# A retention and mixture-of-experts kernel on one core: a weight piece, a chunk's scaling and the last eviction are moved

## The chip, the cores and the metric

The kernel runs on one core of one Trainium2 chip. The metric is the device time of one execution in microseconds (us); the median of three timed executions before the change is 379.56 us (379.56 to 379.77).

## The reference

A retention layer (4 batches, 8 heads, 768 positions, head size 64) feeds a mixture of 8 experts. Every token goes to the one expert with the largest gate logit.

```python
for t in range(S):
    state = gamma[None, :, None, None] * state + np.einsum('bhd,bhe->bhde', k[:, :, t], v[:, :, t])
    y[:, :, t] = scale * np.einsum('bhd,bhde->bhe', q[:, :, t], state)
...
logits = x @ w_gate
expert_idx = np.argmax(logits, axis=1)
...
    h = np.maximum(xe @ w1[e], 0.0)
    ye = h @ w2[e]
    out[mask] = gate_w[mask, None] * ye
```

x is y with its heads side by side: 3072 tokens of 512 numbers. w1 is 512x1024 and w2 1024x512 for each expert.

## The kernel before

The work is written out by hand in one order; each engine executes its own instructions in the order in which the code issues them, and waits where data or a buffer is missing.

**Attention.** The 3072 tokens are 24 chunks of 128, taken two at a time in 12 periods (n = 0 to 11; period n has the chunks a = 2n and b = 2n+1). In a period TensorE adds the carried state to Y (`carry`), forms the gate logits of the period before (`logits`, `finish_logits`), turns that period's rows (`rows`), updates the state U (`update`), adds the chunk's own part to Y (`output`), and computes the next period's scores. VectorE evicts Y times a decay into xT (`evict`) and the masked scores into Sb. GpSimd scales v into vs (`scale`; chunk g's vs is read by `update(g)` and `output(g)`). Y has one buffer, so the carry of the next period waits until both evictions are done.

**Sending.** Once a chunk's slots are known, GpSimd sends its 128 rows to the expert regions of x_sorted in HBM by an indirect DMA (`send_apart`, one DMA for each chunk, with `between()` after each but the last; by default `between` is `pause`, a small multiplication whose result nobody reads). `soon` is period 9: there chunks 16 and 17 are sent, and SyncE then reads the first 240 rows of the first expert back (`fetch_early` into xg0), which can only start when every row sent so far has landed. In period 11 VectorE turns xg0 into xt (`turn_early`, L868), ScalarE casts it into xh (`cut_high`, L875), and TensorE starts the first expert's hidden layer with it (`fill`, L908).

**Weights.** Raw float32 weights are split into a high part (ScalarE, `whi`) and a rest (`wlo`) in pieces; SPLITS[7] are the three pieces of period 7, whose rests VectorE computes.

**Experts.** From about 98 us on TensorE runs the experts; the eighth one's last block of 120 tokens is computed in two halves of 256 columns (`last_rows`). Each half is evicted from its own bank of PSUM with the gate weight as a factor and sent to the output by GpSimd. The execution ends when the second of these DMAs has landed.

## Time and profile before

| | |
|---|---|
| timed executions | median 379.56 us, 379.56 to 379.77 |
| profiled execution | 379.4 us, span 377.6 us |
| TensorE (PE) busy | 371.0 us, 98% of the span |
| VectorE (DVE) busy | 251.7 us, 67% |
| GpSimd (POOL) busy | 260.3 us, 69% |
| ScalarE (ACT) busy | 140.5 us, 37% |
| granted TensorE clock | 0.997 of full speed |

The span runs from the first to the last instruction of the program; 1.8 us of the profiled execution lie around it. TensorE's ends are modelled, so that a short wait between two matmuls can be hidden in its busy time; the starts are recorded.

### The profile page before, as it was taken

Reading aid. Unit: us, or ns where it says so; the run is one execution under the profiler, and the core shown is the slowest. Engines: PE = TensorE matmul, PEld = TensorE weight load, DVE = VectorE, ACT = ScalarE, POOL = GpSimd, SP = SyncE. Lnnn points to the kernel's source line nnn. Section 1 sums busy time; section 2 is a strip of 40 time slices with the busy share of each in tenths; the row PEclk is TensorE's granted clock in tenths of the full one; section 3 lists DMA queues with packets and bytes.
Section 4 is the critical chain, followed back from the end, with each engine's and each line's share of the span. In section 5 each row is a group of like instructions: output and inputs, shape, how many; then the busy total and the mean of one; then the engine's idle time right before and its main releaser. Section 6 shows DMA issues by size and latency. Waiting matters only on the chain. (4 is left out here: it accounts for less than half of the span.)

```text
span 377.6 us, 8710 instructions
## 1 busy us (share of the span) xinstructions
PE 371.0 (98%) x3279; PEld 349.3 (93%) x3279; DVE 251.7 (67%) x496; ACT 140.5 (37%) x252; POOL 260.3 (69%) x278
## 2 busy tenths in 40 slices
PE   8999999999999999999999999999999999999994
PEld 5888888788899899999999999999999999999984
DVE  3467858877778866768784777576676668667211
ACT  2222344244541645534630543154235316424200
POOL 3751669988760299008996999499569929987873
PEclk9999999999999999999999999999999999999998
DMA  7999999986249597869646754846457557520102
GB/s 305 417 414 420 416 402 423 417 353 172 92 159 201 197 240 252 262 217 277 223 145 115 231 162 141 194 166 210 133 149 224 176 91 251 184 101 24 38 20 80
DMA packets 42031, 82.06 MB, mean 217 GB/s; under 512 B 4268, under 2 KB 17584, under 8 KB 39537
## 3 DMA queue, kind: packets, MB, share of 16 engines
q1 hardware_dynamic: 36656, 67.67, 54.4%
q0 software_dynamic: 5312, 13.49, 10.0%
q8 instruction: 47, 0.77, 0.9%
q14 instruction: 16, 0.12, 0.1%
HBM read 65.80 MB, written 15.85 MB: 216 GB/s over the span
## 5 line engine op out<-in xcount | busy, mean ns | idle before, releaser
L853 POOL DMA_INDIRECT out<-Z,sidx x88 | 100.9, 1147 | 63.9 <-DVE Z L1061 49.2
L148 DVE TENSOR_TENSOR wlo<-raw,whi 128x1024 fp32r<-128x1024 f32 (+1 forms) x63 | 74.0, 1178 | 16.5 <-ACT whi L147 16.2
L203 POOL TENSOR_TENSOR idle<-cs 1x256 bf16<-1x256 f32 x102 | 79.6, 780 | 2.8
L147 ACT CAST whi<-raw 128x1024 fp32r<-128x1024 f32 (+1 forms) x72 | 67.7, 951 | 5.8 <-DMA raw<-w 5.8
L1218 PE MATMUL py<-hh,whi 128*128 128x392 f32 (+4 forms) x192 | 65.7, 342 | 0.0
L1218 PE MATMUL py<-hl,whi 128*128 128x392 f32 (+4 forms) x192 | 65.7, 342 | 0.0
L1218 PE MATMUL py<-hh,wlo 128*128 128x392 f32 (+4 forms) x192 | 65.7, 342 | 0.0
L1193 ACT ACTIVATE hh<-ph 128x452 fp32r<-128x452 f32 (+6 forms) x56 | 28.4, 507 | 77.6 <-PE ph L1186 77.1
L1186 PE MATMUL ph<-xh,wlo 128*128 128x392 f32 (+5 forms) x224 | 49.0, 340 | 0.0
L1186 PE MATMUL ph<-xl,whi 128*128 128x392 f32 (+5 forms) x224 | 48.9, 340 | 0.0
L1186 PE MATMUL ph<-xh,whi 128*128 128x392 f32 (+5 forms) x224 | 48.9, 340 | 0.0
L1194 DVE SCALAR_TENSOR_TENSOR hl<-ph,hh 128x452 fp32r<-128x452 f32 (+6 forms) x56 | 32.1, 574 | 20.3 <-ACT hh L1193 19.5
L1186 PEld LDWEIGHTS ph<-xh,whi 128*128 128x128 f32 x224 | 40.2, 188 | 0.4
L1186 PEld LDWEIGHTS ph<-xl,whi 128*128 128x128 f32 x224 | 40.3, 188 | 0.2
L1186 PEld LDWEIGHTS ph<-xh,wlo 128*128 128x128 f32 x224 | 40.2, 188 | 0.1
L1218 PEld LDWEIGHTS py<-hl,whi 128*128 128x128 f32 x192 | 36.1, 188 | 0.2
L1218 PEld LDWEIGHTS py<-hh,wlo 128*128 128x128 f32 x192 | 36.1, 188 | 0.2
L1218 PEld LDWEIGHTS py<-hh,whi 128*128 128x128 f32 x192 | 36.0, 188 | 0.2
L287 DVE TENSOR_TENSOR Sb<-sp,cs 128x512 f32<-128x512 f32 x48 | 29.9, 681 | 5.9 <-PE sp L284 5.9
L875 ACT CAST xh<-buf 128x512 fp32r<-128x512 f32 (+6 forms) x24 | 13.3, 558 | 51.5 <-DVE buf L868 51.5
L853 POOL DMA_INDIRECT x_sorted<-xrow,KEY x24 | 24.9, 1037 | 6.9 <-issue 4.1
L1056 DVE STREAM_TRANSPOSE Z<-py 128x416 f32<-128x416 f32 (+3 forms) x24 | 15.0, 625 | 18.9 <-PE py L1218 18.5
(200 smaller groups left out, 555.6 us busy)
## 6 DMA issues: line engine op xcount, KB each, us to landing
raw<-w SPq DMA_DIRECT2D x32, 1024.0 KB, 6.1
qkv_w<-qkv SPq DMA_DIRECT2D x12, 1024.0 KB, 17.7
qkv_t<-qkv SPq DMA_DIRECT2D x7, 1024.0 KB, 15.1
qkv_t<-front SPq DMA_DIRECT2D x7, 512.0 KB, 7.5
buf<-x_sorted SPq DMA_DIRECT2D x12, 211.2 KB, 5.2
x_sorted<-cs SPq DMA_DIRECT2D x7, 260.0 KB, 5.5
buf<-x_sorted SPq DMA_DIRECT2D x8, 195.0 KB, 3.9
out<-Z,sidx POOLq DMA_INDIRECT x88, 3.6
```

What stands on the lines that cost most here:

```text
L147: nc.scalar.copy(out=hi[:, h], in_=raw[:, h])
L148: engine.tensor_tensor(out=lo[:, h], in0=raw[:, h], in1=hi[:, h].bitcast(F32), op=ALU.subtract)
L203: nc.gpsimd.tensor_tensor(out=idle[0:1], in0=cs[0:1, 0:PAUSE], in1=cs[0:1, 0:PAUSE], op=ALU.mult)
L287: nc.vector.tensor_tensor(out=Sb[:, r], in0=sps[r], in1=causal.unsqueeze(1).broadcast_to([P, NP, C]), op=ALU.mult)
L853: sc = tc.nc.gpsimd.indirect_dma_start(out=dst, out_offset=bass.IndirectOffsetOnAxis(ap=index, axis=0), in_=rows, in_offset=None, bounds_c ...
L875: nc.scalar.copy(out=xh[:, :, c0:c0 + w], in_=xt[:, :, t0:t0 + w])
L1056: nc.vector.transpose(out=Zs[e][:, 0:nb, k, :], in_=py[:, 0:32 * nb].rearrange("p (j c) -> p j c", c=32))
L1186: nc.tensor.matmul(out=ph[:, :w], lhsT=wparts[e, f // 4][a][:, kd, fo:fo + P], rhs=x[:, kd, :w], start=(n == 0), stop=(n == 3 * KD - 1))
L1193: nc.scalar.activation(out=hh[:, :cap], in_=ph[:, :cap], func=AF.Relu)
L1194: nc.vector.scalar_tensor_tensor(out=hl[:, :cap], in0=ph[:, :cap], scalar=0.0, in1=hh[:, :cap].bitcast(F32), op0=ALU.max, op1=ALU.subtract)
L1218: nc.tensor.matmul(out=py[:, :c], lhsT=a[:, f % 4, k * P:(k + 1) * P], rhs=x[:, :c], **se)
```

## The change

Three edits. In period 7 the third weight piece is split after the two evictions, where it was split before them. In period 9 the scaling of chunk 21 stands between the sends of chunks 16 and 17, where a pause stood; it stood behind the second send. And each half of the last eviction is shared: VectorE takes 128 of its 256 columns and ScalarE the other 128.

```diff
-            for i in SPLITS[n][1:] if n == 7 else ():
+            for i in SPLITS[n][1:2] if n == 7 else ():
                 split(0, *i, nc.vector, 1)
...
-                send_apart(range(FULL - 2, FULL))
+                send_apart(range(FULL - 2, FULL), lambda: scale(b + 2))
                 fill_late()
                 fetch_early()
...
             for g in (a, b):
                 evict(g)
+            for i in SPLITS[n][2:] if n == 7 else ():
+                split(0, *i, nc.vector, 1)
...
-                if n not in BEHIND:
+                if n not in BEHIND and n != soon:
                     scale(b + 2)
...
-            nc.vector.tensor_scalar(out=half.rearrange("p (o k r) -> p k o r", o=2, k=KD),
-                                    in0=py[:w, 0:DM // 2].rearrange("p (k o r) -> p k o r", o=2, k=KD),
-                                    scalar1=meta[:w, j, 1:2], scalar2=None, op0=ALU.mult)
+            src = py[:w, 0:DM // 2].rearrange("p (k o r) -> p k o r", o=2, k=KD)
+            dst = half.rearrange("p (o k r) -> p k o r", o=2, k=KD)
+            by = meta[:w, j, 1:2]
+            nc.vector.tensor_scalar(out=dst[:, :, 0], in0=src[:, :, 0], scalar1=by, scalar2=None, op0=ALU.mult)
+            nc.scalar.activation(out=dst[:, :, 1], in_=src[:, :, 1], func=AF.Copy, scale=by)
             scatter_rows(tc, out_halves, pair[:w, q:q + 1], half, "rows")
```

On VectorE, in period 7 (wlo is a weight piece's rest, xT an eviction of Y, Sb the masked scores):

```order
 L287 TENSOR_TENSOR Sb<-sp,cs 128x512 x4
 L408 TENSOR_REDUCE lg_1120<-lp 128x16
-L148 TENSOR_TENSOR wlo<-raw,whi 128x512 x3
-L345 TENSOR_TENSOR xT<-Y,buf 128x4x128 x2
+L148 TENSOR_TENSOR wlo<-raw,whi 128x512 x2
+L345 TENSOR_TENSOR xT<-Y,buf 128x4x128 x2
+L148 TENSOR_TENSOR wlo<-raw,whi 128x512
 L287 TENSOR_TENSOR Sb<-sp,cs 128x512 x4
 L408 TENSOR_REDUCE lg_1120<-lp 128x16
```

Both evictions stand one piece earlier; the scores' evictions still stand behind three pieces and two evictions.

On GpSimd, at the sends of chunks 15, 16 and 17, before (idle is the pause, vs a chunk's scaling):

```order
L853 DMA x_sorted<-xrow,KEY 25600x520
L203 TENSOR_TENSOR idle<-cs 1x256
L853 DMA x_sorted<-xrow,KEY 25600x520 x2
L203 TENSOR_TENSOR idle<-cs 1x256
L853 DMA x_sorted<-xrow,KEY 25600x520
L261 TENSOR_TENSOR vs<-qkv_t,cs 128x512 x2
L148 TENSOR_TENSOR wlo<-raw,whi 128x512 x2
```

and of the change:

```order
L203 TENSOR_TENSOR idle<-cs 1x256
L855 DMA x_sorted<-xrow,KEY 25600x520 x2
L261 TENSOR_TENSOR vs<-qkv_t,cs 128x512
L855 DMA x_sorted<-xrow,KEY 25600x520
L261 TENSOR_TENSOR vs<-qkv_t,cs 128x512
L148 TENSOR_TENSOR wlo<-raw,whi 128x512 x2
```

The pause in front of the last of these sends (chunk 17) is gone, and the first of the two scalings (chunk 21) stands in its place.

On ScalarE, at the program's end, of the change, each row with the engines whose semaphores it waits for (hh is the hidden layer, yo the output rows, py the bank of PSUM):

```order
L1197 ACTIVATE hh<-ph_2196 128x376 [waits DVE_49,PE_49]
L1046 ACTIVATE yo<-py_2192,meta_97 120x128 [waits DMASW4_49,DVE_49]
L1046 ACTIVATE yo<-py_2193,meta_97 120x128 [waits DVE_49]
L841 TENSOR_LOAD top [waits DVE_49]
L842 COMPARE_AND_BRANCH
```

and on GpSimd, there, of the change:

```order
L855 DMA out<-yo,sidx_101 3072x512 [waits DMASW4_49,DVE_49]
L203 TENSOR_TENSOR idle<-cs 1x256 [waits Pool_49]
L855 DMA out<-yo,sidx_101 3072x512 [waits DMASW5_49,DVE_49]
L855 DMA out<-yo,pair 6144x256 [waits DMASW6_49,Activation_49]
L855 DMA out<-yo,pair 6144x256 [waits DMASW7_49,Activation_49]
```

ScalarE's two evictions are new. They wait for VectorE and not for TensorE, and the last two DMAs, which waited for VectorE, wait for ScalarE.

## Rows read from the trace of the kernel before

**Rows 1.** The page's part 1: busy time, share of the span, instructions.

```profile
PE 371.0 (98%) x3279; PEld 349.3 (93%) x3279; DVE 251.7 (67%) x496; ACT 140.5 (37%) x252; POOL 260.3 (69%) x278
```

**Rows 2.** Waits of TensorE: us in total, times, longest us.

```profile
PE U L301 <- POOL vs L261: 0.3, 1, 0.3
PE Y L323 <- DVE xT L345: 0.3, 1, 0.3
```

**Rows 3.** Timeline of PE, 56 to 98 us: start, us, what, [idle before <-releaser].

```profile
61.72 0.38 PE L402 MATMUL lp<-cs,LT 128*128 128x128 f32 x2
62.03 0.69 PE L301 MATMUL U<-vs,qkv_t 128*64 128x64 f32 x16
...
64.86 2.06 PE L284 MATMUL sp<-qkv_t 64*128 64x128 f32 x32
67.23 1.10 PE L323 MATMUL Y<-qkv_t,ub 64*64 64x128 f32 x32 [0.32 <-DVE xT L345]
...
85.02 0.38 PE L402 MATMUL lp<-cs,LT 128*128 128x128 f32 x2
85.73 0.69 PE L301 MATMUL U<-vs,qkv_t 128*64 128x64 f32 x16 [0.33 <-POOL vs L261]
...
88.97 2.06 PE L284 MATMUL sp<-qkv_t 64*128 64x128 f32 x32
90.96 1.10 PE L323 MATMUL Y<-qkv_t,ub 64*64 64x128 f32 x32
...
95.70 0.71 PE L908 MATMUL ph<-xh,whi 128*128 128x240 f32 x4
```

**Rows 4.** Timeline of DVE, 65.3 to 68 us.

```profile
65.21 0.68 DVE L148 TENSOR_TENSOR wlo<-raw,whi 128x512 fp32r<-128x512 f32 x1
65.81 1.27 DVE L345 TENSOR_TENSOR xT<-Y,buf 128x512 f32<-128x512 f32 x2
```

**Rows 5.** Timeline of POOL, 64.3 to 69.5 us.

```profile
64.89 1.31 POOL L853 DMA_INDIRECT x_sorted<-xrow,KEY  x1 [0.16 <-issue]
66.22 0.60 POOL L203 TENSOR_TENSOR idle<-cs 1x256 bf16<-1x256 f32 x1
66.98 1.02 POOL L853 DMA_INDIRECT x_sorted<-xrow,KEY  x1 [0.16 <-issue]
```

**Rows 6.** Timeline of POOL, 81.6 to 91 us.

```profile
82.82 0.60 POOL L203 TENSOR_TENSOR idle<-cs 1x256 bf16<-1x256 f32 x1
83.58 1.01 POOL L853 DMA_INDIRECT x_sorted<-xrow,KEY  x1 [0.16 <-issue]
84.62 2.05 POOL L261 TENSOR_TENSOR vs<-qkv_t,cs 128x512 f32<-128x512 f32 x2
```

**Rows 7.** Timeline of the DMA queue of SP, 81 to 91 us.

```profile
87.10 2.96 SPq L157 DMA_DIRECT2D xg<-x_sorted  x4
```

**Rows 8.** Waits of SP, 81 to 91 us (the longest lies behind that window).

```profile
SPq L157 <- DMA x_sorted<-xrow,KEY: 21.1, 2, 19.9
```

**Rows 9.** DMA issues, 97 to 109 us: median us to landing.

```profile
x_sorted<-xrow,KEY POOLq DMA_INDIRECT x6, 2.9
```

**Rows 10.** Timeline of all engines, 93.3 to 95.75 us.

```profile
92.96 1.30 DVE L868 STREAM_TRANSPOSE xt<-xg 128x512 f32<-128x512 f32 x2 [0.18 <-DMA xg<-x_sorted]
...
93.71 1.16 ACT L875 CAST xh<-xt 128x512 fp32r<-128x512 f32 x2 [0.58 <-DVE xt L868]
```

**Rows 11.** Timeline of DVE, 367.1 us to the end.

```profile
367.14 0.75 DVE L1017 TENSOR_SCALAR yo<-py,meta 128x512 f32<-128x512 f32 x1 [4.80 <-PE py L1216]
...
372.80 0.48 DVE L1040 TENSOR_SCALAR yo<-py,meta 120x256 f32<-120x256 f32 x1 [2.34 <-PE py L1034]
```

**Rows 12.** Timeline of POOL, 369.9 us to the end.

```profile
373.58 1.01 POOL L853 DMA_INDIRECT out<-yo,pair  x1 [1.80 <-DVE yo L1040]
```

**Rows 13.** Groups of ACT by line and shape: busy us, mean ns, idle before.

```profile
L304 ACT COPY ub<-U 128x256 f32<-128x256 f32 x20 | 7.4, 372 | 15.8 <-PE U L301 15.8
L499 ACT COPY xrow<-GW 128x8 f32<-128x8 f32 x4 | 0.8, 204 | 6.4 <-DVE GW L494 6.4
```

## The prediction

> **What bounds the kernel now.** The page's busy times come first: TensorE is busy for 98% of the span [rows 1], so only what lets TensorE start something earlier, or what lies behind its last matmul, can move the time. The view of waits, asked for TensorE alone, then has two lines of 0.3 us beside one at the program's start [rows 2]: the carry of period 8 waits for VectorE's eviction xT, and an update of U waits for GpSimd's vs. The changed code touches both. The timeline gives them their place and size, and here the reader should compare starts, since the ends are modelled [rows 3]. From the start of 32 score matmuls to the carry behind them TensorE takes 90.96 - 88.97 = 1.99 us where nothing is late, but 67.23 - 64.86 = 2.37 us at the end of period 7: a stall of 0.38 us. From the last transpose of logits to the update it takes 62.03 - 61.72 = 0.31 us, but 85.73 - 85.02 = 0.71 us at chunk 21: 0.40 us. Behind 98 us no wait of TensorE is listed. What it has won by then should therefore reach the end, unless work that does not move with it becomes late.

> **Edit 1, the weight piece.** VectorE's third piece starts at 65.21 and the first eviction at 65.81, so the evictions move forward by one piece, 0.60 us, more than the stall; their input, Y, is complete by then, since TensorE is already at the scores [rows 3, 4]. The carry would start 0.38 us earlier. The piece itself lands between the evictions and the four score evictions, which keep their place; its result is needed by the first expert alone. It costs something elsewhere: a rest computed by VectorE from two inputs in SBUF hinders GpSimd. The send that begins at 64.89 takes 1.31 us with such pieces beside it, the next one 1.02 us [rows 5]. The moved piece now lies beside the pause at 66.22 and the send at 66.98. Either GpSimd loses nothing (the piece is over) or 0.3 us, as that send did; I take 0.2 us, because the evictions, 0.60 us earlier, end at 67.08 - 0.60 = 66.48, and a piece of 0.68 us behind them covers the start of the send at 66.98. TensorE does not feel this at once.

> **Edit 2, the scaling.** A pause costs 0.60 us and a scaling 2.05 / 2 = 1.03 us [rows 6]. Chunk 21's vs is ready at about 85.68 now; in the pause's place it is ready at 82.82 + 1.03 = 83.85, or 84.05 with the 0.2 us of edit 1. TensorE asks for it at 85.73 - 0.40 - 0.38 = 84.95, so the stall of 0.40 us is gone, and with it the limit that would have swallowed the gain of edit 1: GpSimd does not get earlier through edit 1, so that alone would only lengthen this wait. Together TensorE is 0.78 us early. Chunk 22's scaling comes out earlier too, by the missing pause.

> What is late next: the send of chunk 17 starts 1.03 - 0.60 = 0.43 us later, 0.63 us with the 0.2 us above. Behind it SyncE waits for all sends to land before it fetches xg0 [rows 8]; that fetch starts at 87.10 now, 3.5 us after this send began at 83.58 [rows 6, 7]. Behind the fetch VectorE turns xg0 (92.96, after a wait for that transfer) and ScalarE casts it until 93.71 + 1.16 = 94.87 [rows 10]; with some 0.14 us for the release (the eviction that ended at 65.81 + 1.27 = 67.08 let the carry start at 67.23 [rows 3, 4]) TensorE could start the first expert at 95.01. It does at 95.70 [rows 3], so this chain has 0.69 us to spare before the change, and TensorE's 0.78 us would use up all of it. With the fetch later by D, what is left of TensorE's gain is the smaller of 0.78 and 0.69 - D us. D lies between 0 and 0.63. The bound of 0 comes from the sends behind 97 us, which land 2.9 us after their start [rows 9]: 83.58 + 0.63 + 2.9 = 87.11, as now. I take 0.15 us, near that end: an estimate that the 0.6 us between 3.5 and 2.9 are a queue that is being worked off, which a later send finds shorter. Left: 0.54 us.

> **Edit 3, the last eviction.** Now VectorE takes 0.48 us for 120x256, and GpSimd's send starts 373.58 - 372.80 = 0.78 us after VectorE did, 0.30 us behind its end [rows 11, 12]. After the change the two halves are not side by side. In the listed order ScalarE's part waits for VectorE and not for TensorE; the only way in which it can learn that its bank is complete is through VectorE's part of the same bank. So the path is VectorE, then ScalarE, then GpSimd. VectorE for 128 columns: 0.75 us for 512 and 0.48 us for 256 give 0.27 us for each 256, so 0.35 us. ScalarE for 128: between 0.37 us for 256 and 0.20 us for 8 columns [rows 13], 0.29 us by a straight line. A hand-over from VectorE to ScalarE takes about 0.1 us or less: the first of the two transposes ends some 0.65 us behind 92.96, and ScalarE starts at 93.71 [rows 10]; I take 0.05 us. Sum: 0.35 + 0.05 + 0.29 + 0.30 = 0.99 us in place of 0.78: a loss of 0.2 us. Bounds: with 0.24 us (half of 0.48) and 0.20 us nothing is lost; with 0.48 and 0.37 us 0.4 us are. The first half's send only moves inside the time in which TensorE computes the second half, so it costs nothing.

> [...]

> **Sum.** -0.54 + 0.2 = -0.34 us, against the profiled execution's own 379.4 us, which is 0.16 us under the median of 379.56. A difference should carry over to the median: 379.2 us.

> **Rivals.** Differences under 0.2% (0.76 us) are about what a measurement of this kernel cannot tell from no change.

> (A) The fetch is later by as much as the send, D = 0.63 us. For it: the same landing of 3.5 us behind the send. Then 0.06 us of TensorE's gain is left, and with the tail the time is 379.56 - 0.06 + 0.2 = 379.7 us.

> (B) The fetch is not later (D = 0) and the tail costs nothing, or even gains because ScalarE's part does run beside VectorE's: then the longer of 0.35 and 0.29 us replaces 0.48, a gain of 0.13 us. -0.69 + 0 = 378.9 us, or -0.69 - 0.13 = 378.7 us. Against the second: the listed waits.

> (C) Slower: the fetch of xg0 gets much later than the send, because its own four issues are slow (they take 2.96 us from first to last [rows 7]) or the send lands late. It decides from 0.69 us on, from where TensorE starts the first expert later than before; the kernel is slower by 0.2% where 0.69 - D - 0.2 = -0.76, so from D = 1.25 us, and at D = 1.5 it takes 380.6 us. Against it: in the rows the landings get shorter, not longer, with time [rows 9].

> (D) The change does nothing at TensorE, because the evictions are held up in period 7 by something else than the piece, and vs is not what ends the wait at 85.73. Then only the tail is left: 379.8 us. Against it: both releasers are named in the rows and the starts fit [rows 3].

> **How the numbers follow.** Forecast 379.2 us, 5 in 10; (A) 2 in 10; (B) 15 in 100; (C) 1 in 10; (D) 5 in 100. Faster by over 0.2% means under 378.80 us: about two thirds of (B), and the end of the forecast where the tail costs nothing, 0.15 together. Slower by over 0.2% means over 380.32 us: (C) and little else, 0.1. The rest, 0.75, is within 0.2%. The range holds the forecast, (A), (D) and (B) down to 378.6 us, where the bounds of the tail, of D and 0.1 us of scatter meet; upward 379.9 us, (D) with the same scatter.

> **What would show it.** In the profile after: the carry of period 8 starts 1.99 us behind the scores, without the wait for xT; chunk 21's update starts 0.31 us behind the transposes; the send of chunk 17 starts about 0.4 to 0.6 us later, and the fetch of xg0 tells D; TensorE's first matmul on xh comes 0.5 us earlier, right behind ScalarE's cast, now with a wait for it. At the end ScalarE's part starts when VectorE's ends, and the send starts 1.0 us behind VectorE. The prediction is wrong if D is far from 0.15 us, if the two parts of the eviction overlap, or if a new wait of TensorE appears behind 98 us.

## The result and the profile after

| | before | after |
|---|---|---|
| timed executions (22 each) | median 379.53 us, 379.36 to 379.89 | median 382.63 us, 379.32 to 383.43 |
| ratio | | 1.0068, 95% interval 1.0052 to 1.0083 |
| profiled execution | 379.40 us, span 377.6 us | 383.35 us, span 381.6 us |

The change makes the kernel 0.7% slower (the ratio goes by all the executions; the medians alone lie 3.1 us, 0.8%, apart). 379.2 us was forecast, and the range ended at 379.9 us. The wide spread after the change belongs to the finding: two executions took 379.3 and 379.4 us, the other twenty 380.7 to 383.4 us. The profiled execution is one of the three slowest, so what is read from it below explains such an execution.

The view of waits of TensorE, after (us in total, times, longest), stands against [rows 2]:

```profile
PE ph L910 <- ACT xh L877: 2.9, 1, 2.9
PE warm L576 <- DVE ones L170: 1.1, 1, 1.1
PE U L301 <- DMA head<-second_rows: 0.3, 1, 0.3
```

The two stalls of 0.3 us are gone. In their place is one of 2.9 us, at the first expert's first matmul. (The other two lie at the program's start: the wait of 1.1 us is there before the change too, and the one of 0.3 us ends at 7.56 us at an update that TensorE reached at 7.71 us before.) The timeline of PE, after, for [rows 3]:

```profile
64.99 2.06 PE L284 MATMUL sp<-qkv_t 64*128 64x128 f32 x32
66.97 1.10 PE L323 MATMUL Y<-qkv_t,ub 64*64 64x128 f32 x32
...
84.92 0.38 PE L402 MATMUL lp<-cs,LT 128*128 128x128 f32 x2
85.23 0.69 PE L301 MATMUL U<-vs,qkv_t 128*64 128x64 f32 x16
...
93.31 1.97 PE L336 MATMUL Y<-Sb,vs 128*64 128x128 f32 x32
98.17 1.21 PE L910 MATMUL ph<-xh,whi 128*128 128x240 f32 x4 [2.89 <-ACT xh L877]
...
104.50 0.37 PE L933 MATMUL acc<-hh,whi 128*128 128x256 f32 x1
```

From scores to carry 66.97 - 64.99 = 1.98 us, from logits to update 85.23 - 84.92 = 0.31 us: both gains are there. But the matmul on xh starts at 98.17 in place of 95.70, 2.47 us late, and the row at 104.50 stood at 100.73 before (timeline of PE, before):

```profile
100.73 0.36 PE L931 MATMUL acc<-hh,whi 128*128 128x256 f32 x1
```

That is 3.77 us late, and so it stays up to the last eviction (376.57 against 372.80). Why the delay grows is in the view by stages, after (stretch, its length, busy time of PE, PEld, DVE, ACT and POOL with the number of instructions, granted clock, DMA share, GB/s):

```profile
93.00:95.00 2.00, 2.00 (x35) 1.83 (x34) 0.00 (x0) 0.00 (x0) 1.76 (x2) 1.00 0.80 218
95.00:97.00 2.00, 0.28 (x6) 0.03 (x2) 0.79 (x2) 0.05 (x1) 0.00 (x0) 1.00 0.84 319
97.00:99.00 2.00, 0.83 (x4) 0.84 (x5) 2.00 (x5) 2.00 (x5) 1.28 (x1) 0.79 0.03 12
99.00:101.00 2.00, 2.00 (x12) 1.45 (x15) 1.83 (x8) 0.91 (x3) 1.27 (x1) 0.50 0.00 0
101.00:103.00 2.00, 2.00 (x21) 1.41 (x14) 0.55 (x3) 1.36 (x6) 1.70 (x3) 0.86 0.17 64
103.00:105.00 2.00, 2.00 (x26) 1.97 (x25) 0.69 (x2) 0.73 (x3) 0.92 (x1) 1.00 0.44 171
```

The third figure from the right is the clock: behind the idle time TensorE is granted 0.50 of full speed from 99 to 101 us. The same four matmuls on xh take 1.21 us where they took 0.71 [rows 3]. From there to the row at 104.50 TensorE takes 6.33 us in place of 5.03, which costs 3.77 - 2.47 = 1.30 us more.

Where the 2.9 us come from is read backwards. The timelines of GpSimd and of SyncE's DMA queue, after, for [rows 5 to 7]:

```profile
66.34 0.60 POOL L203 TENSOR_TENSOR idle<-cs 1x256 bf16<-1x256 f32 x1
67.11 1.28 POOL L855 DMA_INDIRECT x_sorted<-xrow,KEY  x1 [0.16 <-issue]
...
83.20 1.08 POOL L261 TENSOR_TENSOR vs<-qkv_t,cs 128x512 f32<-128x512 f32 x1
84.45 1.01 POOL L855 DMA_INDIRECT x_sorted<-xrow,KEY  x1 [0.17 <-issue]
```

```profile
89.29 2.34 SPq L157 DMA_DIRECT2D xg<-x_sorted  x4
91.90 0.40 SPq L139 DMA_DIRECT2D raw<-w  x1
```

Chunk 17's send starts 0.87 us later than before, xg0's fetch 2.19 us later. The semaphore events of that send tell where the difference lies. Before, its 16 completions came at 86.19 to 86.36 (13 of them) and 86.99 to 87.08 (3). After, 15 come at 87.06 to 87.25, only 0.2 us behind the last ones of before, and one comes at 89.28. SyncE, which waits for this send, starts at 89.29, 0.01 us behind the sixteenth; before, it started at 87.10, 0.02 us behind the sixteenth at 87.08.

What kept the sixteenth is in the view of DMA, after, from 86.88 to 88.1 us (packets, MB, share of 16 engines' time), where the core's DMA engines start a single packet:

```profile
DMA packets 1, 0.02 MB, mean 13 GB/s; under 512 B 0, under 2 KB 0, under 8 KB 0
...
q8 instruction: 1, 0.02, 6.3%
```

6.3% is one sixteenth: one DMA engine is busy for the whole stretch, with 16,384 bytes of instructions (86.89 to 88.12 in the packet records). In the next stretch, 88.1 to 89 us, the send's last two packets of 4,160 bytes (88.10 and 88.54) and its completion mark (88.79) run:

```profile
q0 software_dynamic: 3, 0.01, 4.9%
```

All its other packets were over by 86.88. The same happens again to xg0's own transfers: another 16,384 bytes of instructions run at 93.18 for 1.14 us, 15 engines complete the last two transfers by 93.8 and 94.2, the sixteenth at 95.48 and 96.08. So xg0 is whole at 96.08 in place of 92.84, 3.24 us late.

The end of the program, after (timeline of DVE, ACT and POOL), for [rows 11, 12]:

```profile
376.57 0.35 DVE L1045 TENSOR_SCALAR yo<-py,meta 120x128 f32<-120x128 f32 x1 [2.47 <-PE py L1036]
376.95 0.37 ACT L1046 ACTIVATE yo<-py,meta 120x128 f32<-120x128 f32 x1 [2.46 <-DVE yo L1045]
377.62 1.01 POOL L855 DMA_INDIRECT out<-yo,pair  x1 [1.80 <-DVEq L842]
```

The parts run one behind the other, and the send starts 377.62 - 376.57 = 1.05 us behind VectorE's start, 0.78 before: 0.27 us lost. 2.47 + 1.30 + 0.27 = 4.04 us, against 4.0 us between the spans.

### The profile page after: what moved, and what is told of

The parts are those of the page before. It is cut to its first block, busy times and chain, and to the rows that moved or that the text cites. A ratio compares the mean times of both kernels' runs of the same rounds, so it can differ in the third digit from the quotient of the medians.

```text
span 381.6 us, 8712 instructions
## 1 busy us (share of the span) xinstructions
PE 372.1 (98%) x3279; PEld 349.8 (92%) x3279; DVE 252.9 (66%) x496; ACT 141.1 (37%) x254; POOL 260.1 (68%) x277
## 5 line engine op out<-in xcount | busy, mean ns | idle before, releaser
L855 POOL DMA_INDIRECT out<-Z,sidx x88 | 99.7, 1133 | 63.7 <-DVE Z L1065 49.0
L148 DVE TENSOR_TENSOR wlo<-raw,whi 128x1024 fp32r<-128x1024 f32 (+1 forms) x63 | 74.8, 1190 | 14.8 <-ACT whi L147 14.6
```

Source lines behind the costliest of these rows:

```text
L148: engine.tensor_tensor(out=lo[:, h], in0=raw[:, h], in1=hi[:, h].bitcast(F32), op=ALU.subtract)
L855: sc = tc.nc.gpsimd.indirect_dma_start(out=dst, out_offset=bass.IndirectOffsetOnAxis(ap=index, axis=0), in_=rows, in_offset=None, bounds_c ...
```

## Experiments

The theory from here on: chunk 17's last packets meet an instruction fetch of TensorE on one DMA engine. Packet records don't name their engine, so that the fetch and the late packets share one, and that the fetch is TensorE's, has to be shown otherwise. The rivals: the send's lateness is passed on whatever the instruction fetch does, or TensorE's own lead of 0.78 us makes xg0 late.

**The edits apart.** e1 has only the moved piece, e2 only the moved scaling, e3 both, e4 only the shared eviction:

```diff
e1, e3:
-            for i in SPLITS[n][1:] if n == 7 else ():
+            for i in SPLITS[n][1:2] if n == 7 else ():
...
             for g in (a, b):
                 evict(g)
+            for i in SPLITS[n][2:] if n == 7 else ():
+                split(0, *i, nc.vector, 1)
e2, e3:
-                send_apart(range(FULL - 2, FULL))
+                send_apart(range(FULL - 2, FULL), lambda: scale(b + 2))
...
-                if n not in BEHIND:
+                if n not in BEHIND and n != soon:
```

e4 is the last part of the change's diff. Expected of e1: 

> Edit 1 alone (the third weight piece behind the evictions). Theory: the 3 us come from chunk 17's send, which starts later, so that its last packets on one DMA engine fall behind an instruction fetch of 16 KB at about 86.9 us; the xg0 fetch then starts 2 us later and TensorE idles. Edit 1 delays this send by 0.3 us alone: its last packets end at about 86.56 + 0.3 = 86.86 us, mostly before the instruction fetch, so 379.5 us with single slow runs; TensorE's 0.38 us at period 7 is lost again waiting for vs at chunk 21's update. Rival: the xg0 fetch is slow because TensorE comes earlier and with it its own instruction fetches; then edit 1 alone does nothing either: 379.5 us, without any slow run.

Of e2: 

> Edit 2 alone (chunk 21's scaling in the pause's place). Theory: the send starts 0.43 us later, its last packets end at about 87.0 us and meet the instruction fetch in most runs: xg0 fetch at about 89 us, TensorE idle for 2 us or more, 381 to 382.5 us, with some runs at 379.2 us. Rival: TensorE is only 0.4 us earlier, half of the lead, so half of the loss or none: 379.2 to 380.5 us.

Of e3: 

> Edits 1 and 2 without the shared eviction. Theory and rival: as the whole change but for the end, where the eviction before takes 0.27 us less: 382.4 us, spread from 379 to 383.2 us.

Of e4: 

> Edit 3 alone (the last eviction shared). Theory: VectorE's 0.35 us and ScalarE's 0.37 us follow each other, 1.05 us from VectorE's start to the send in place of 0.78: 379.8 us. Rival (the first half's send or the branch at the end hides it): 379.5 us.

The kernel before took 379.71 us beside them (379.36 to 381.42).

| | median, us | range | ratio, 95% interval |
|---|---|---|---|
| e1, piece | 380.06 | 379.66 to 380.55 | 1.0002, 0.9991 to 1.0014 |
| e2, scaling | 379.42 | 378.99 to 380.25 | 0.9990, 0.9979 to 1.0002 |
| e3, both | 381.03 | 379.02 to 383.18 | 1.0035, 1.0013 to 1.0058 |
| e4, eviction | 380.11 | 379.61 to 381.29 | 1.0009, 0.9997 to 1.0020 |

Neither edit alone is measurably slower; together they are, with the change's wide spread, though by less than expected (381.03 us for 382.4). For e2 the theory had expected the slowdown, and missed. e1 decides nothing between theory and rival: they differ only in whether single executions take longer, and e1's longest (380.55 us) is under that of the kernel before beside it (381.42 us). In e1 the wait for vs grew, as the prediction had it for this edit alone (timeline of PE):

```profile
86.17 0.69 PE L301 MATMUL U<-vs,qkv_t 128*64 128x64 f32 x16 [0.80 <-POOL vs L261]
```

In e2 the send starts at 84.33, its last packet is over at 86.75, the instruction fetch starts at 86.74, and all 16 engines land by 87.18: a near miss. In e3 the send starts at 84.74, packets run until 87.17 and the fetch at 86.84; 15 engines land by 87.54, one at 88.97. That execution took 379.39 us nevertheless, because none of xg0's own transfers then had a late engine, and they were whole at 93.97 (timelines of SyncE's queue and of PE, e3):

```profile
88.98 2.34 SPq L157 DMA_DIRECT2D xg<-x_sorted  x4
```

```profile
96.05 0.72 PE L910 MATMUL ph<-xh,whi 128*128 128x240 f32 x4 [0.48 <-ACT xh L877]
```

So the first collision alone makes TensorE wait for 0.5 us and leaves the clock alone (the four matmuls take 0.72 us, and the granted clock is 1.00 from 94 to 104 us); the waits of 2.9 us (after) and 2.4 us (f1 below, where one engine completes xg0 at 95.51 and the others by 93.99) have the second one as well. No run separates the second from the first on purpose, and each kernel has one profile, so that the spread of its other executions is laid to the same collisions without being shown.

**Send earlier, fetch earlier, send later.** e5 has edits 1 and 2, and the sends of chunks 14 to 17 earlier by one pause; e8 has edit 2 and the last send later by one pause; e6 and e7 leave the send alone and shift TensorE's instructions, by 12 small matmuls at the program's start in the kernel before, and 40 in the changed one:

```diff
e5:
-                    pause()
                     send_behind(ubs[(a + 2) % 3][:, 0, 0:1], AFTER[n])
...
e8:
+                send_apart(range(FULL - 2, FULL), lambda: (scale(b + 2), pause()))
e6 (12), e7 (40):
         keep_warm(WARM)
+        for i in range(40):
+            nc.tensor.matmul(out=warm[:, 0:64], lhsT=ones, rhs=ones[:, 0:64], start=True, stop=True)
```

Of e5: 

> Edits 1 and 2 as in the change, without edit 3, and without the pause ahead of the sends of chunks 14 to 17, so that these four sends start 0.6 to 0.8 us earlier than in the change. Theory (the last packets of chunk 17's send wait behind a 16,384-byte fetch of instructions at 86.9 us that uses the same DMA engine): the send starts at about 83.8, its last packet is over before 86.9, all 16 engines have landed by 87.2, xg0's fetch starts at 87.1 or so, TensorE keeps 0.5 us or more of its 0.78 us; 378.7 to 379.2 us, with no run above 380.5. Rival (TensorE's own lead is what makes xg0 late, whatever the send does): still 380.5 to 382 in the median, with the wide spread of the change.

Of e6: 

> The kernel before with 12 small matmuls (64 columns, result unread) added behind the warm-up at the program's start, where TensorE waits for its first data anyway. Nothing else moves, but TensorE's instruction fetches should come 12 matmuls earlier, the one of 86.9 us at about 86.2, inside the packets of chunk 17's send. Theory: one of the 16 engines lands 1 to 2 us late, xg0's fetch starts at 88 to 89 us in place of 87.1, TensorE waits for xh by 1 us or more: 380.5 to 382.5 us, though no edit was made. Rival (the send's start or TensorE's lead decides): 379.5 to 379.9 us as before, xg0's fetch at 87.1.

Of e7: 

> The changed kernel with 40 such small matmuls at the program's start, so that the instruction fetch of 86.9 us comes at about 84.6 us and is over when chunk 17's last packets run. Theory: the send that starts at 84.45 lands whole by 87.3, xg0's fetch starts at about 87.3, TensorE's idle time of 2.9 us is gone, unless the next instruction fetch (at about 91) meets xg0's own transfers and costs up to 1 us; 378.9 to 380 us. Rival: 382 to 383 us as the change, xg0's fetch at 89.

Of e8: 

> Edit 2 alone, with one pause more between the scaling of chunk 21 and the send of chunk 17, so that this send starts 0.6 us later than in edit 2 alone (at about 84.9 us). Theory: its last packets (87.3) now run into the instruction fetch at 86.8; landing and xg0's fetch at 88.8 to 89.3 us, 1.7 us or more behind 87.2 for a send that is 0.6 us later; 380.5 to 382 us. Rival (lateness in proportion): xg0's fetch at 87.8 us, 379.5 to 380 us.

On the chip of these four the kernel before itself took 381.39 us (380.69 to 382.38). e5 took 381.54 us (1.0003, 0.9994 to 1.0012), e6 381.70 (1.0007, 0.9998 to 1.0016), e7 381.26 (0.9992, 0.9982 to 1.0001), e8 382.55 (1.0036, 1.0013 to 1.0060; 380.60 to 384.71).

Neither the change nor e2 was run on this chip, so the times of e7 and e8 have only the kernel before beside them, and the traces carry the argument. e5 and e6 miss their aim. In e5 TensorE stalls elsewhere (timeline of PE, e5), for no reason that the profile names, and with it the sends:

```profile
81.15 0.36 PE L301 MATMUL U<-vs,qkv_w 128*64 128x64 f32 x5 [0.26 <-issue]
81.90 0.36 PE L301 MATMUL U<-vs,qkv_w 128*64 128x64 f32 x5 [0.40 <-issue]
```

Chunk 17's send starts at 85.45 in e5 and at 85.03 in e6, the instruction fetches come at 88.78 and 88.31, behind the packets, and neither shows a late engine. They say only that a later send by itself lands 2.8 us behind its start. e7's trace speaks for the theory, with all three edits in, though its time misses what was expected (378.9 to 380 us): the fetch runs from 85.03 to 86.31, the send's 16 engines land within 88.23 to 88.44, and TensorE has no wait at xh. So does e8 (timeline of SyncE's queue, waits of TensorE):

```profile
89.99 2.34 SPq L157 DMA_DIRECT2D xg<-x_sorted  x4
```

```profile
PE ph L908 <- ACT xh L875: 1.7, 1, 1.7
```

With edit 2 alone, a send started at 85.33 runs into a fetch of 1.37 us at 87.44; 15 engines land by 88.12, one at 89.97. With the 2.8 to 2.9 us behind the send that e2, e5, e6 and e7 show, the fetch of xg0 would have come at 88.2. The second collision is there too, but shorter (xg0 is whole at 95.81, on 15 engines at 95.14), and this wait of 1.7 us shows no loss of clock: the mean granted in the profiled execution is 0.998, where it is 0.995 after the change and 0.997 before.

**The instruction fetch alone.** To shift the fetch without lengthening the program's start, 5 of the 8 warm-up matmuls are replaced by 40 small ones in the same time; f1 is the change once more, f2 the change, f3 the kernel before and f4 edits 1 and 2 with this start:

```diff
-WARM = 8
+WARM = 3
...
+        for i in range(40):
+            nc.tensor.matmul(out=warm[:, 0:64], lhsT=ones, rhs=ones[:, 0:64], start=True, stop=True)
```

Of f1: 

> The changed kernel itself once more, as the reference for the three runs beside it. Theory (the last packets of chunk 17's send, and then xg0's own transfers, wait behind TensorE's instruction fetches at 86.9 and 93.2 us): slower than before by 0.3 to 0.9%, with runs up to 1% slower than the best, on this chip too. Rival (the slowdown belongs to one chip): within 0.2% of before.

Of f2: 

> The changed kernel with all three edits; at the program's start 3 of the 8 warm-up matmuls are left, with 40 matmuls of 64 columns behind them in the time of the other 5, so that 35 matmuls more stand ahead of all that follows and TensorE's instruction fetches come about 2 us earlier (near 85 us in place of 86.9). Theory: no fetch runs while the send's last packets do, so all 16 engines land within 0.3 us of each other, xg0's fetch starts within 3.0 us of the send's start, TensorE idles less than 0.5 us at xh, and the time is at least 1 us (0.3%) under that of the changed kernel beside it and not above the kernel before. Rival (the send's later start, or TensorE's earlier arrival, makes xg0 late whatever the instruction fetch does): within 0.3 us of the changed kernel beside it.

Of f3: 

> The kernel before with the same start (3 warm-up matmuls and 40 small ones): the control. Theory: its send met no fetch anyway, so it stays within 0.2% of the kernel before. Rival (the new start is itself faster or slower): then it differs from the kernel before by as much as the change with that start differs from the change.

Of f4: 

> Edits 1 and 2 without edit 3, with that start. Theory: what the prediction gave the two edits (0.5 to 0.8 us) is kept, with no slow runs, and edit 3's 0.3 us are saved: 0.1 to 0.25% faster than the kernel before, 0.2 to 0.4 us under the version with all three edits. Rival: as slow as edits 1 and 2 were (0.35% slower), with a spread of 3 us or more.

| kernel before: 379.70 us | median, us | range | ratio, 95% interval |
|---|---|---|---|
| f1, the change | 381.69 | 379.48 to 382.65 | 1.0037, 1.0019 to 1.0054 |
| f2, the change, fetch shifted | 380.43 | 379.83 to 380.89 | 1.0015, 1.0006 to 1.0024 |
| f3, before, fetch shifted | 380.55 | 379.82 to 382.07 | 1.0025, 1.0015 to 1.0035 |
| f4, edits 1 and 2, fetch shifted | 380.01 | 378.95 to 380.85 | 1.0005, 0.9996 to 1.0014 |

The control f3 missed its expectation, and with it f2 and f4 miss theirs against the kernel before: the new start itself costs 0.85 us (f3's profile, of its fastest execution, shows 0.5 of them at the last eviction, 0.4 from a wait of TensorE for hl at 119 us; the rest stays open). Against it the change is no longer slower (380.43 against 380.55), and edits 1 and 2 gain 380.55 - 380.01 = 0.54 us. That this is just what the prediction had left of TensorE's gain is luck: each of the two intervals reaches nearly 0.4 us to either side. 35 more matmuls of TensorE are the only edit that moved the fetch from 86.9 us to 84.93 in f2 and 84.69 in f3, so it is TensorE's. In f2 the send starts later than in the change, and lands sooner. The view of DMA from 86.5 to 88.6 us holds the send and no instructions, and the next views are the timeline of SyncE's queue and the waits of TensorE from 56 to 98 us (f2):

```profile
DMA packets 84, 0.28 MB, mean 133 GB/s; under 512 B 17, under 2 KB 17, under 8 KB 84
...
q0 software_dynamic: 84, 0.28, 35.1%
```

```profile
88.55 2.34 SPq L157 DMA_DIRECT2D xg<-x_sorted  x4
```

```profile
PE ph L912 <- ACT xh L879: 0.2, 1, 0.2
```

f1 beside it has this wait with 2.4 us, and its xg0 fetch at 89.14. The moved fetch (84.93 to 86.31) now holds up chunk 16's send instead: 15 of its engines complete by 86.73, one at 87.86. That costs nothing here, since chunk 17's send lands later still, at 88.53. f4 shows the same (86.47 and 87.43).

**The repair.** e5's kernel again where the kernel before takes its usual time (379.76 us), and as its control the earlier sends alone. Of g1: 

> Edits 1 and 2 without edit 3, and without the pause ahead of the sends of chunks 14 to 17; where the kernel before takes 379.7 us, so on another chip than e5. Theory (collision of the send's last packets with the instruction fetch): the send of chunk 17 starts near 83.8 us, all engines have landed by 87.2, xg0's fetch starts at about 87.2, no wait of TensorE at xh over 0.3 us; 379.0 to 379.4 us, highest run under 380.5. Rival (TensorE's lead makes xg0 late): 380.5 to 381.5 us with runs up to 383, as edits 1 and 2 alone.

Of g2: 

> The kernel before without the pause ahead of the sends of chunks 14 to 17 and nothing else: the control for g1. Theory: these sends start 0.7 us earlier, TensorE still has its stalls of 0.38 and up to 0.40 us, so nothing is gained: 379.5 to 379.9 us, 0.4 to 0.8 us above g1. Rival: as fast as g1, if the earlier sends are what gains.

g1 takes 379.13 us (378.77 to 379.61; 0.9978, 0.9969 to 0.9987), g2 379.21 us (379.01 to 379.66; 0.9987, 0.9978 to 0.9996). g1 is faster than the kernel before beside it, and its longest execution is shorter than that kernel's median; the change took 382.63 and 381.69 us where it ran. The rival falls, since TensorE leads here too. Rows of g1 (timelines of PE and of SyncE's queue):

```profile
65.02 2.06 PE L284 MATMUL sp<-qkv_t 64*128 64x128 f32 x32
67.01 1.10 PE L323 MATMUL Y<-qkv_t,ub 64*64 64x128 f32 x32
...
84.96 0.38 PE L402 MATMUL lp<-cs,LT 128*128 128x128 f32 x2
85.27 0.69 PE L301 MATMUL U<-vs,qkv_t 128*64 128x64 f32 x16
```

```profile
87.26 2.38 SPq L157 DMA_DIRECT2D xg<-x_sorted  x4
```

Of g2 I had expected nothing, and its rival came true: it is as fast as g1 within the noise (the medians differ by 0.08 us, and the intervals overlap). Its scaling of chunk 21 also comes earlier, and the second stall is gone there too (85.44 - 85.13 = 0.31 us). So g1 shows that an earlier send takes the loss away, and not that edits 1 and 2 then gain anything over the earlier sends alone. In the profiles g1's lead over [rows 3] is 0.47 us at 95.23, but 0.24 us at 98.31, where VectorE's xl takes 1.60 us in place of 1.21 and TensorE waits for it, and 0.18 us at the last eviction; g2's is 0.29, 0.21 and 0.12 us.

All profiled executions in one table. "On time" is the end of the send's last packet without the late ones.

| | send 17 starts | on time until | instruction fetch | last engine | xg0 fetch, behind the send |
|---|---|---|---|---|---|
| g2 | 83.12 | 86.54 | 86.51 to 87.60 | 87.05 | 87.06, 3.9 |
| before | 83.58 | 86.57 | 86.91 to 88.25 | 87.08 | 87.10, 3.5 |
| e4 | 83.59 | 86.63 | 86.95 to 88.02 | 87.14 | 87.16, 3.6 |
| f3 | 83.73 | 86.72 | 84.69 to 85.71 | 87.24 | 87.26, 3.5 |
| g1 | 83.86 | 86.72 | 86.88 to 87.84 | 87.24 | 87.26, 3.4 |
| e1 | 84.02 | 86.73 | 87.15 to 88.35 | 87.25 | 87.26, 3.2 |
| e2 | 84.33 | 86.75 | 86.74 to 87.73 | 87.18 | 87.20, 2.9 |
| e6 | 85.03 | 87.45 | 88.31 to 89.27 | 87.84 | 87.86, 2.8 |
| f4 | 85.14 | 87.59 | 84.66 to 86.07 | 88.11 | 88.12, 3.0 |
| e5 | 85.45 | 87.88 | 88.78 to 89.73 | 88.28 | 88.29, 2.8 |
| f2 | 85.53 | 88.01 | 84.93 to 86.31 | 88.53 | 88.55, 3.0 |
| e7 | 85.62 | 88.04 | 85.03 to 86.31 | 88.44 | 88.46, 2.8 |
| f1 | 84.34 | 86.76 | 86.46 to 87.96 | 89.12 | 89.14, 4.8 |
| after | 84.45 | 86.88 | 86.89 to 88.12 | 89.28 | 89.29, 4.8 |
| e3 | 84.74 | 87.17 | 86.84 to 87.80 | 88.97 | 88.98, 4.2 |
| e8 | 85.33 | 87.75 | 87.44 to 88.81 | 89.97 | 89.99, 4.7 |

In the lower four the fetch runs while the other engines finish (in after it starts 0.01 us behind them), and one engine is late in each. In the upper twelve the fetch is over 1.0 us or more before the send's last packet, or starts at its end at the earliest (0.03 us before it in g2), and no engine is late in this way. That it is one and the same engine shows in the lower four: the first of the late packets starts within 0.02 us of the fetch's end, at 88.10 in after, 87.95 in f1, 87.79 in e3 and 88.80 in e8. After and e2 are close cases that fell out differently, which fits the spread of the executions: some tenths of a microsecond decide.

## Why the prediction was wrong

**The stalls of TensorE (edits 1 and 2): right.** 0.38 and 0.40 us were priced, and both rows fell to 1.98 and 0.31 us. That edit 1 alone only lengthens the wait for vs showed in e1. What the prediction left out is a later loss of the lead: in g1, where nothing collides, the 0.47 us at the first expert's first matmul shrink to 0.18 us by the end, because VectorE's xl is done only 0.08 us earlier (98.16 against 98.24). So the 0.54 us would not have been kept whole even with D as forecast.

**What edit 1 costs GpSimd: right.** The send beside the moved piece takes 1.28 us in place of 1.02, 0.26 us for the 0.2 taken. Chunk 17's send is 0.87 us later, and not 0.63. Of this 0.39 us are there at chunk 16's send already (82.22 against 81.83): the 0.26 us, and 0.13 us by which everything is later ahead of the first edit (scores at 64.99 against 64.86). The scaling in the pause's place adds 0.48 us (2.23 us from send to send, 1.75 before) for the 0.43 taken. The moved piece is held up as well: beside the send it takes 0.96 us, and not the 0.68 us of the prediction.

**The delay D of xg0's fetch: the step that failed.** 0.15 us was taken, with 0.63 as its upper bound; it was 2.19 us at the start of the fetch and 3.24 us at its end, because one engine is late again (96.08, the other 15 by 94.20); no term of the sum stood for that. The bound rested on landings of other sends and supposed that a landing can be later by no more than the send is. For 15 of the 16 engines the estimate was good (0.2 us). The sixteenth stood behind an instruction fetch that starts 0.34 us behind the send's last packet before the change, a margin that the packet records of before show and that the prediction did not weigh. After the change that fetch runs from 86.89 to 88.12, none of the send's packets starts between 86.88 and 88.10, and its last two run from 88.10 on.

**The slack of 0.69 us: right.** 3.24 - 0.69 = 2.55 us, and TensorE came 2.47 us later.

**Rival (C): the mechanism, with a tenth of the chance.** "The send lands late" is what happened; that the four issues are slow is not (2.34 us, 2.96 before). With D = 3.24 its sum gives 379.56 + 2.55 + 0.2 = 382.3 us. That this is near the median of 382.63 us is partly luck: the rival lacked the clock, 1.30 us, priced nowhere, and with it the sum is 383.6 us, for a profiled execution of 383.35.

**The tail: right, a little small.** 0.27 us for 0.2, since ScalarE takes 0.37 us and not 0.29. e4's profile shows the same 1.05 us (373.87 - 372.82), but its ratio can't tell this from nothing.

## What to carry to other kernels

A transfer that another engine waits for is as late as the slowest of its 16 DMA engines (here 89.28 us, with the other 15 done at 87.25): before such a transfer is moved by half a microsecond, look at what else runs there, the instruction queues too, and how far off it is. Bounding a landing by the landings of other transfers is safe only while nothing new lies in its way (here the bound was 0.63 us, and xg0's fetch came 2.19 us later). And a wait of TensorE is to be priced with the stretch at the lower clock that can follow it: here 1.30 us behind the wait of 2.9 us, half as much again as TensorE came late, and nothing behind those of 0.5 and 1.7 us (e3, e8).
